# Two attention blocks in one kernel: value tiles cut in halves by heads, a separate stretch for each query tile of the last turn, and another written order of the work

## The chip, the cores and the metric

One core of one Trainium2 chip runs the whole kernel. The metric is the device time of one execution in microseconds. Three runs of the kernel before are shown, and one more execution was taken with the hardware profiler on.

## The reference

Two attention blocks work on 2048 tokens of width 640 each, with 32 heads of 20 columns. Their outputs stand side by side in a result of 2048 x 1280. Everything is bf16.

```
# A: four segments of 512 tokens, one after the other
logits = q @ k.T * 20**-0.5 + where(query < key, -1e9, 0)   # causal within a segment
a_dot  = softmax(logits) @ v
a_mem  = phi(q) @ M / (phi(q) @ z + 1e-6)       # phi(t) = t+1 if t > 0 else exp(t)
out    = (sigmoid(beta) * a_mem + (1 - sigmoid(beta)) * a_dot) @ wo
M += phi(k).T @ v ;  z += sum(phi(k))           # memory of the segments before
# B: sliding window, a query sees itself and the 255 keys before it
out    = softmax(where(0 <= i - j < 256, q @ k.T * 20**-0.5, -1e9)) @ v @ wo
```

## The kernel before

The work is cut into eight chunks of 512 tokens, which alternate: A0, B0, A1, B1, A2, B2, A3, B3 (numbers 0 to 7). For each chunk q and k are projected in five pieces of 128 columns (q, k with 32 rows per head of which 20 are the head's; the columns of the last heads are packed into the unused rows, written to DRAM and read back into groups 5 to 7), v in two halves of 16 heads, four token tiles each. Heads go in 8 groups of four. Scores are computed transposed (keys on partitions), 153 batches of up to 2 x 1024 columns in three two-bank tiles `sc`; ScalarE takes their exponentials into ten `pt` tiles (line 830), GpSimd (869) and VectorE (847) mask the edges. A value group (`av`, line 883; in the last chunk `av_tile`, line 904, by query tiles) multiplies the weights with v, which carries a column of ones for the sums. The result is transposed by 32 x 32 blocks on VectorE (949), divided on GpSimd (987), collected in `o`, written to DRAM, turned by a DMA transpose (1040) and projected with wo (935). In block A from segment 1 on a memory group is added (`mem`).

The matmuls of the projections, the value groups and the memory all go through two one-bank PSUM tiles `m0` and `m1`, used in turn. The output projections of the end use `sc` tiles too.

The values: `vA` (block A) and `vB0`, `vB1` (block B, by turns) are tiles of 128 partitions x 4 token tiles x 696 columns, which hold both halves of the heads of a chunk (line 789, `v_tile`). `vS` holds copies of vA with its 64-token blocks placed otherwise, `vL`, `vU` and `vX` copies of parts of vB for the edges of the window: `vL` the lower 64 tokens of each tile, `vU` the upper ones, `vX` the first tile with the other half from the chunk before. SyncE makes these copies by DMA (lines 757 and 783). For a chunk of B but the first, half 0 issues first the two carries from the chunk before (`vU` and `vX`, both halves of the heads at once), then three copies of its own half; half 1 issues three.

The turned rows: all chunks but the last turn their rows into `oT`; the last one, by query tiles, into a tile `xT` of 128 x 5 x 576, where query tile t takes the columns 128 t to 128 t + 127 of each of the five pieces (lines 1037 to 1041). Its last query tile is turned by matmuls instead (`last_job`).

What sets the order: TensorE runs in the order of the string `PLAN` (line 61). Each word is one step: `q20*5` five matmuls of q of chunk 2 from piece 0 on, `k`, `v`, `o` likewise (`v21`: half 1 of chunk 2; `o70`, `o71`, `o72`: query tiles of chunk 7), `S` or `s` one score batch, `A` one value group, `M` one memory group, `d2` a step of the update of the memory before chunk 2, `z0` the last query tile. After `S` the 128-column matmuls up to the next `A` are issued as four of 32 columns (`by_tiles`, line 930), after `s` as one. The order of the other engines follows from a planner (`Flow`, lines 96 to 267) that keeps a clock for each engine with fixed costs, releases an eviction, mask, division or DMA when it thinks that its input is there, and starts TensorE's next step when it thinks that it can. Only the order of the instructions comes from it; on the chip every engine runs its own list and waits on semaphores. A DMA waits also for the eighth one before it (eight lanes).

At the start SyncE loads x of chunk 0, pieces of the weights wk_A and wq_A (the first pieces on ScalarE's queue), beta, and wv_A in two halves, in this order. VectorE fills vL, vU and vX with zeros, GpSimd sets the ones of vA and vB.

Of the kernel before, what the change touches and what calls it, by code (L numbers as in the profile page):

```python
# [13 lines left out]
P = 128  # L14
# [253 lines left out]
class _K:  # L268
# [391 lines left out]
    def dm_job(self, seg, pkT, v):  # L660
# [12 lines left out]
        for some in (own, [(lambda kt, h=h: spare[:, kt, R2 * h:R2 * h + R2], R2,  # L673
                            [x for x in range(4) if MEM2[x][0] == h], None) for h in (1, 0)]):
            if some is not own:
                yield there
            yield "bank"
            dM, bi = self.bank()
            at = 0
            for lhs, rows, xs, g0 in some:  # L680

                gs = [g0] if g0 is not None else sorted(MEM2[x][1] for x in xs)
                n = W * len(gs)
                v0 = at_head(4 * gs[0])
                for kt in range(LT):
                    nc.tensor.matmul(dM[0:rows, at:at + n], lhsT=lhs(kt),  # L686
                                     rhs=v[:, kt, v0:v0 + n],
                                     start=(kt == 0), stop=(kt == LT - 1))
# [26 lines left out]
    def v_job(self, n, half, w_ap, v, gate, needs):  # L715
# [5 lines left out]
        for tt in range(LT):  # L721
            yield "bank"
            ps, bi = self.bank()
            for kt in range(self.KT):
                self.wide(ps, xT[:, kt, x0 + tt * P:x0 + (tt + 1) * P],
                          w_ap[:, half, kt, :], 320, kt == 0, kt == self.KT - 1)
                if kt < self.KT - 1:
                    yield 0.0
            src = ps[:, 0:320].rearrange("p (h e) -> p h e", e=DH)
            dst = v[:, tt, HV * half:HV * half + 16 * VS].rearrange(  # L730
                "p (h e) -> p h e", e=VS)[:, :, 0:DH]
            if gate:
                nc.vector.tensor_tensor(
                    out=dst, in0=src,
                    in1=self.omg[:, 16 * half:16 * half + 16].unsqueeze(2)
                    .to_broadcast([P, 16, DH]), op=ALU.mult)
# [10 lines left out]
    def v_squares(self, n, half, v):  # L747
# [3 lines left out]
        s = slice(HV * half, HV * half + HV)  # L751
        tok = v[0:SH, :, s].rearrange("p (a b) c -> p a b c", b=2)
        t = f.dve + 138.0

        def go():
            for odd in (0, 1):
                self.nc.sync.dma_start(
                    out=self.vS[SH * odd:SH * odd + SH, odd * 2:odd * 2 + 2, s],
# [6 lines left out]
    def v_ends(self, n, c, half, v):  # L765
# [4 lines left out]
        s = slice(HV * half, HV * half + HV)  # L770
# [18 lines left out]
    def v_tile(self, name, now=True):  # L789
        v = self.big.tile([P, LT, VW], BF16, name=name)  # L790
        if now:
            self.v_ones(v)
        return v

    def v_ones(self, v):
        self.nc.gpsimd.memset(
            v[:].rearrange("p t (x c) -> p t x c", x=2)[:, :, :, 0:16 * VS].rearrange(
                "p t x (h e) -> p t x h e", e=VS)[:, :, :, :, DH], 1.0)
        for c0 in (HV - 12, VW - 12):
            self.nc.gpsimd.memset(v[:, :, c0:c0 + 12], 1.0)  # L800
# [73 lines left out]
    def av(self, parts, g, vof):  # L874
# [4 lines left out]
        for n_, (ref, q0, nq, c0, pts) in enumerate(parts):  # L879
            v = vof(ref)  # L880
            for j in range(4):
                h = 4 * g + j
                nc.tensor.matmul(O[HD * j:HD * j + HD, q0:q0 + nq],  # L883
                                 lhsT=v[:, at_head(h):at_head(h) + HD],
# [7 lines left out]
    def av_tile(self, parts, qt, g0, vof):  # L892
# [3 lines left out]
        for gi in range(4):  # L896
            own = sorted((p[:5] for p in parts[g0 + gi] if p[1] // P == qt),
                         key=lambda e: -e[2])
            for n_, (ref, q0, nq, c0, pts) in enumerate(own):
                v = vof(ref)  # L900
                o0 = gi * P + q0 - qt * P
                for j in range(4):
                    h = 4 * (g0 + gi) + j
                    nc.tensor.matmul(O[HD * j:HD * j + HD, o0:o0 + nq],  # L904
                                     lhsT=v[:, at_head(h):at_head(h) + HD],
# [107 lines left out]
    def final(self, n, o, scr, wo, out2d, r0, col, t0, t1, t):  # L1013
# [19 lines left out]
        def turn(tl):  # L1033
            if n not in self.oT:
                if n == len(self.chunks) - 1:

                    self.oT[n] = self.big.tile([P, self.KT, XC], BF16, name="xT", bufs=2)
                else:
                    self.oT[n] = self.big.tile([P, self.KT, L], BF16, name="oT", bufs=2)
            nc.sync.dma_start_transpose(out=self.oT[n][:, :, t0 * P:t1 * P],  # L1040
# [7 lines left out]
    def final_job(self, n, wo, out2d, r0, col, t0, t1, there):  # L1048
# [4 lines left out]
        for tt in range(t0, t1):  # L1053
            if n == len(self.chunks) - 1 and tt == LT - 2:

                row = r0 + tt * P
                for hf in range(2):
                    yield "bank"
                    self.last_half(hf, lambda m: oT[:, m, tt * P:(tt + 1) * P], wo,
                                   out2d[row:row + P], col)  # L1060
# [7 lines left out]
            lhs = lambda m: oT[:, m, tt * P:(tt + 1) * P]  # L1068
# [235 lines left out]
    def body(self, xA, A_wq, A_wk, A_wv, A_wo, A_beta, xB, B_wqkv, B_wo, out2d):  # L1304
# [39 lines left out]
        self.vL = big.tile([P, LT, VW], BF16, name="vL")  # L1344
        self.vU = big.tile([P, LT, VW], BF16, name="vU")
        self.vX = big.tile([P, VW], BF16, name="vX")
        self.vA = self.v_tile("vA")
        self.vS = big.tile([P, LT, VW], BF16, name="vS")
        self.consts_mz()
        nc.vector.memset(self.vL[:].bitcast(F32), 0.0)  # L1350
        for t in (self.vU, self.vX):
# [6 lines left out]
        nc.gpsimd.memset(self.vS[:].bitcast(F32), 0.0)  # L1358
# [209 lines left out]
    def one_group(self, n, kind, c, g, what, parts, left, o_t, groups_done, scro, wo, out2d):  # L1568
# [3 lines left out]
        def vof(ref):  # L1572
            what, u = ref
            if what == "a":
                return self.vA[:, u, :]
            if what in "st":
                return self.vS[:, 2 * (u % 2) + u // 2, :]
            if what == "l":
                return self.vL[:, u % LT, :]
            if what == "u":  # L1580
                return self.vU[:, u + 2, :]
            if u == 0:
                return self.vX[:]
            return self.vB[c % 2][:, u, :] if u > 0 else self.vB[(c - 1) % 2][:, LT + u, :]
# [128 lines left out]
```

## Time and profile before

| what | value |
| --- | --- |
| median of 3 runs | 329.36 us (328.75 to 333.11) |
| profiled execution | 329.68 us, of which the span is 328.0 us |
| TensorE clock granted | 1.00 throughout |
| DMA packets | 76266, 47.45 MB, mean 145 GB/s |
| score exponentials on ScalarE | 306 of mean 1024 ns |
| GpSimd masks | 512 of mean 376 ns |
| 32 x 32 transposes on VectorE | 88 of mean 709 ns |

The span runs from the first to the last instruction; the rest of an execution lies around it. The profile names a group of instructions by its line, engine and operation and by what it writes and reads (`m<-xT,wBq`). PE is TensorE's matmuls and PEld its weight loads, DVE is VectorE, ACT ScalarE, POOL GpSimd, SP SyncE, and a q behind the name is the queue that issues DMAs. A list of waits gives, for an engine's line and what it waited for, the total in us, how many times, and the longest. "Issue" is time in which the engine waited for nothing that the profile shows. Matmuls are pipelined, so a busy share of TensorE includes overlap.

### The profile page before, as it was taken

How to read it: one execution, taken by the hardware profiler on the slowest of the kernel's cores; microseconds unless marked ns; L12 is line 12 of the kernel's file. 1: busy time of each engine (PE TensorE's matmuls, PEld its weight loads, DVE VectorE, ACT ScalarE, POOL GpSimd, SP SyncE). 2: the span in 40 equal slices, each digit the busy share in tenths (PEclk: the TensorE clock that was granted, in tenths of full speed). 3: DMA queues.
4: the chain of work that ended last, by engine and by line, in shares of the span. 5: the costliest groups of instructions: out<-in, count | busy, mean ns of one | idle time of the engine just before them, and what ended most of it. 6: DMA issues, size and time to landing. Idle time of an engine off the chain costs nothing. (4 is left out here: it accounts for less than half of the span.)

```text
span 328.0 us, 16968 instructions
## 1 busy us (share of the span) xinstructions
PE 315.8 (96%) x7195; PEld 176.3 (54%) x7195; DVE 255.6 (78%) x533; ACT 299.5 (91%) x333; POOL 265.3 (81%) x672
## 2 busy tenths in 40 slices
PE   8999999999999999999999999999999999999995
PEld 2454546555544455555654545456655445666663
DVE  6777767789877887998877897988776788876763
ACT  2979999999999998989999999899999999979982
POOL 8466689998769899977885999998976899998761
PEclk9999999999999999999999999999999999999999
DMA  7975845773689566164689146116968126587752
GB/s 207 400 253 124 199 142 90 162 199 64 137 222 182 108 161 180 38 138 145 142 218 170 28 87 156 52 26 133 156 184 194 26 48 157 141 203 186 119 122 88
DMA packets 76266, 47.45 MB, mean 145 GB/s; under 512 B 48382, under 2 KB 73182, under 8 KB 76190
## 3 DMA queue, kind: packets, MB, share of 16 engines
q1 hardware_dynamic: 75469, 45.71, 58.5%
q8 instruction: 56, 0.92, 1.2%
q10 hardware_dynamic: 720, 0.66, 0.7%
q14 instruction: 21, 0.16, 0.2%
HBM read 17.62 MB, written 16.96 MB: 105 GB/s over the span
## 5 line engine op out<-in xcount | busy, mean ns | idle before, releaser
L830 ACT ACTIVATE pt<-sc 128x1024 bf16<-128x1024 f32 (+2 forms) x306 | 282.5, 1024 | 14.4 <-PE sc L814 12.4
L869 POOL TENSOR_SCALAR_AFFINE_SELECT pt<-pt 128x128 bf16<-128x128 bf16 (+1 forms) x512 | 178.0, 376 | 48.9 <-ACT pt L830 42.0
L949 DVE STREAM_TRANSPOSE tt<-m 128x512 f32<-128x512 f32 x88 | 61.2, 709 | 24.9 <-PE m L883 16.1
L987 POOL TENSOR_TENSOR o<-tt,rr 128x320 bf16<-128x320 f32 x64 | 48.4, 757 | 3.6 <-DVE rr L977 2.6
L814 PE MATMUL sc<-qB,kB 20*64 20x64 bf16 (+2 forms) x1728 | 39.6, 217 | 1.0 <-ACT pt L830 0.3
L935 PEld LDWEIGHTS <-xT 128*128 128x128 bf16 x296 | 26.7, 97 | 18.3 <-issue 6.5
L847 DVE TENSOR_TENSOR pt<-pt,ends 128x1024 bf16<-128x1024 bf16 (+2 forms) x50 | 36.3, 737 | 0.0
L1100 DVE CAST ot<-m 128x320 bf16<-128x320 f32 x58 | 28.1, 486 | 9.4 <-PE m L935 8.2
L814 PEld LDWEIGHTS <-kB 20*64 20x64 bf16 (+1 forms) x1728 | 22.0, 98 | 22.5 <-issue 20.7
L814 PE MATMUL sc<-qA,kA 20*64 20x64 bf16 (+4 forms) x1024 | 33.4, 237 | 0.3 <-ACT pt L830 0.3
L935 PEld LDWEIGHTS <-oT 128*128 128x128 bf16 x244 | 21.4, 97 | 11.9 <-issue 2.6
L814 PEld LDWEIGHTS <-kA 20*128 20x128 bf16 (+1 forms) x1024 | 13.5, 97 | 22.2 <-issue 21.1
L935 PE MATMUL m<-wBv,xT 128*128 128x320 bf16 x147 | 24.2, 299 | 0.9 <-DVE tt L949 0.4
L883 PE MATMUL m<-pt,vA 128*32 128x192 bf16 (+3 forms) x512 | 23.6, 274 | 0.2
L935 PE MATMUL m<-xT,wBq 128*128 128x512 bf16 x82 | 21.4, 380 | 0.3 <-DVE tt L949 0.3
L935 PE MATMUL m<-wo_A,oT 128*128 128x320 bf16 x125 | 21.0, 301 | 0.3 <-DVE kA L557 0.3
L935 PE MATMUL m<-xT,wBk 128*128 128x512 bf16 x81 | 20.7, 381 | 0.0
L935 PE MATMUL m<-wv_A,xT 128*128 128x320 bf16 x119 | 19.8, 300 | 0.7 <-issue 0.5
L738 DVE CAST vB<-m 128x320 bf16<-128x320 f32 x32 | 15.6, 489 | 5.3 <-PE m L935 3.1
L935 PE MATMUL m<-wo_B,oT 128*128 128x320 bf16 x109 | 18.6, 300 | 0.6 <-DVE tt L949 0.4
L557 DVE CAST qB<-m 128x512 bf16<-128x512 f32 x20 | 13.8, 688 | 6.7 <-PE m L935 3.4
L557 DVE CAST kB<-m 128x512 bf16<-128x512 f32 x20 | 13.6, 681 | 6.6 <-PE m L935 5.6
(127 smaller groups left out, 464.1 us busy)
## 6 DMA issues: line engine op xcount, KB each, us to landing
out_dram<-ot SPq DMA_DIRECT2D x29, 160.0 KB
scr_o<-o SPq DMA_DIRECT2D x28, 160.0 KB
xT<-in_B_x_dram SPq DMA_DIRECT2D x8, 288.0 KB
xT<-in_A_x_dram SPq DMA_DIRECT2D x8, 256.0 KB
scr_pk<-e SPq DMA_DIRECT2D x15, 128.0 KB
vS<-vA SPq DMA_DIRECT2D x16, 87.0 KB
vL<-vB SPq DMA_DIRECT2D x8, 174.0 KB
scr_kA<-kA SPq DMA_DIRECT2D x16, 60.0 KB
```

What stands on the lines that cost most here:

```text
L557: nc.vector.tensor_copy(out=dst[:, m, at:at + L], in_=ps[:, :])
L738: nc.vector.tensor_copy(out=dst, in_=src)
L814: nc.tensor.matmul(ps[j // 2][h0:h1, j % 2, c0:c0 + nq], lhsT=k[rows, g, k0:k0 + h1 - h0], rhs=q[rows, g, q0:q0 + nq], start=True, stop=Tr ...
L830: nc.scalar.activation(out=pt[:, :, lo:hi], in_=ps[i][:, :, lo:hi], func=ACT.Exp, scale=self.scale)
L847: nc.vector.tensor_tensor(out=blk, in0=blk, in1=self.ends[:, c0, :].unsqueeze(1).unsqueeze(1) .to_broadcast([P, 2, n // SH, SH]), op=ALU.mult)
L869: nc.gpsimd.affine_select(out=blk, in_=blk, pattern=pat, compare_op=ALU.is_ge, fill=self.zero, base=base, channel_multiplier=mul)
L883: nc.tensor.matmul(O[HD * j:HD * j + HD, q0:q0 + nq], lhsT=v[:, at_head(h):at_head(h) + HD], rhs=pts[j // 2][:, j % 2, c0:c0 + nq], start= ...
L935: self.nc.tensor.matmul(ps[:, 0:n], lhsT=lhsT, rhs=rhs, start=start, stop=stop, skip_group_check=True)
L949: self.nc.vector.transpose(out=tt[:], in_=O[:, :])
L987: nc.gpsimd.tensor_tensor(out=to[:] if add_to else to, in0=a, in1=b, op=ALU.mult)
L1100: nc.vector.tensor_copy(out=ot[:, 320 * hf:320 * hf + 320], in_=ps[:, 0:320])
```

## The change

Three things are done at once.

Value tiles: `vA`, `vB0`, `vB1`, `vS`, `vL`, `vU` and `vX` become two tiles each, one for each half of the heads (348 columns). Readers choose the tile by the group (`g // 4`). The fills at the start become two each. The carries from the chunk before are issued by each half for itself, so that half 1 issues five copies instead of three and half 0's carries are half as large.

Turned rows: in the last chunk, query tile t takes the 640 columns from 640 t on of the flat tile `xT`, so that each query tile has a stretch of its own.

Order: `PLAN` has the same steps in another order, with other places of `S` and `s`.

```diff
 PLAN = (
-    "k00*5 q00*5 k01*4 S k01 q01*5 S v00*16 S v00*4 k02 S k02*4 k03*5 q02*3 S q02*2 q03*5 k04*5 "
+    "q00*5 k00*5 k01*5 v00*4 S v00 q01*5 v00*2 s v00*13 k02 s k02*4 q02*2 s q02*3 k03*3 S k03*2 "
...
-    "v71 s v71*4 A M s v71*10 s A M s o30*10 s o40*5 o30*5 s o30*5 A s o40*10 s o40*10 A o40*5 "
-    "s o40*5 o50*3 s o50*2 o40*5 o50*2 s o50*3 A s o50*10 s A o50*2 s o50*9 s o50*9 s A o60*5 s "
-    "o60*5 o70*5 A o70 s o70*4 o60*5 s o60*5 o71*4 s o71*6 o60*2 s o60*6 A o60*8 A o60*4 o72*2 "
-    "z0*4 ")
+    "v71*3 s v71 o30*5 A s v71*5 M s o40*5 A M s v71*8 s v71*2 o40*5 o30*5 s o40*5 A s o30*10 "
+    "o40*4 s o40*6 A o40*4 s o40*11 s o50*8 s A o50 s o50*11 s A o50 s o50*8 s o50*11 s A "
+    "o60*10 s o60*5 A o70*2 s o70*8 s o60*5 o71*5 s o71*5 o60*5 s o60*5 A o60*6 A o60*4 o72 "
+    "z0*2 o72 z0*2 ")
...
     def v_squares(self, n, half, v):
-        tok = v[0:SH, :, s].rearrange("p (a b) c -> p a b c", b=2)
+        tok = v[half][0:SH].rearrange("p (a b) c -> p a b c", b=2)
...
     def v_ends(self, n, c, half, v):
-        if half == 0 and c > 0:
-            pv = self.vB[(c - 1) % 2]
-            todo += [(self.vU[hi, 0:2, :], pv[hi, 2:4, :], 820.0),
-                     (self.vX[lo, :], pv[lo, 0, :], 410.0)]
-        todo += [(self.vL[lo, :, s], v[lo, :, s], 820.0),
-                 (self.vU[hi, 2:4, s], v[hi, 0:2, s], 410.0),
-                 (self.vX[hi, s], v[hi, 0, s], 205.0)]
+        if c > 0:
+            pv = self.vB[(c - 1) % 2][half]
+            todo += [(vU[hi, 0:2, :], pv[hi, 2:4, :], 410.0), (vX[lo, :], pv[lo, 0, :], 205.0)]
+        todo += [(vL[lo], v[lo], 820.0), (vU[hi, 2:4, :], v[hi, 0:2, :], 410.0),
+                 (vX[hi, :], v[hi, 0, :], 205.0)]
...
+    def half_tiles(self, name, ones=False):
+        ts = [self.big.tile([P, LT, HV], BF16, name="%s%d" % (name, x)) for x in range(2)]
+        for t in ts if ones else ():
+            self.nc.gpsimd.memset(t[:, :, 0:16 * VS].rearrange(
+                "p t (h e) -> p t h e", e=VS)[:, :, :, DH], 1.0)
+            self.nc.gpsimd.memset(t[:, :, HV - 12:HV], 1.0)
+        return ts
...
     def av(self, parts, g, vof):
-            v = vof(ref)
+            v = vof(ref, g // 4)
...
     def final(self, n, o, scr, wo, out2d, r0, col, t0, t1, t):
-                    self.oT[n] = self.big.tile([P, self.KT, XC], BF16, name="xT", bufs=2)
+                    t = self.big.tile([P, self.KT, XC], BF16, name="xT", bufs=2)
+                    flat = t[:].rearrange("p k s -> p (k s)")
+                    self.oT[n] = [flat[:, self.D * x:self.D * x + self.D].rearrange(
+                        "p (k s) -> p k s", k=self.KT) for x in range(LT)]
...
     def body(self, xA, A_wq, A_wk, A_wv, A_wo, A_beta, xB, B_wqkv, B_wo, out2d):
-        self.vL = big.tile([P, LT, VW], BF16, name="vL")
+        self.vL = self.half_tiles("vL")
...
-        self.vB = [self.v_tile("vB0"), self.v_tile("vB1")]
+        self.vB = [self.half_tiles("vB0", True), self.half_tiles("vB1", True)]
```

More of the change, by code (lines that the diff above doesn't have):

```diff
@@ L683, in dm_job @@
                 n = W * len(gs)
-                v0 = at_head(4 * gs[0])
+                v0 = at_head(4 * gs[0]) - HV * (gs[0] // 4)
                 for kt in range(LT):
                     nc.tensor.matmul(dM[0:rows, at:at + n], lhsT=lhs(kt),
-                                     rhs=v[:, kt, v0:v0 + n],
+                                     rhs=v[gs[0] // 4][:, kt, v0:v0 + n],
                                      start=(kt == 0), stop=(kt == LT - 1))
@@ L729, in v_job @@
             src = ps[:, 0:320].rearrange("p (h e) -> p h e", e=DH)
-            dst = v[:, tt, HV * half:HV * half + 16 * VS].rearrange(
+            dst = v[half][:, tt, 0:16 * VS].rearrange(
                 "p (h e) -> p h e", e=VS)[:, :, 0:DH]
@@ L750, in v_squares @@
         f = self.f
-        s = slice(HV * half, HV * half + HV)
-        tok = v[0:SH, :, s].rearrange("p (a b) c -> p a b c", b=2)
+        tok = v[half][0:SH].rearrange("p (a b) c -> p a b c", b=2)
         t = f.dve + 138.0
@@ L757, in go @@
                 self.nc.sync.dma_start(
-                    out=self.vS[SH * odd:SH * odd + SH, odd * 2:odd * 2 + 2, s],
+                    out=self.vS[half][SH * odd:SH * odd + SH, odd * 2:odd * 2 + 2, :],
                     in_=tok[:, :, odd, :])
@@ L769, in v_ends @@
         lo, hi = slice(0, SH), slice(SH, P)
-        s = slice(HV * half, HV * half + HV)
+        vL, vU, vX, v = self.vL[half], self.vU[half], self.vX[half], v[half]
         todo = []
-        if half == 0 and c > 0:
-            pv = self.vB[(c - 1) % 2]
-            todo += [(self.vU[hi, 0:2, :], pv[hi, 2:4, :], 820.0),
-                     (self.vX[lo, :], pv[lo, 0, :], 410.0)]
-        todo += [(self.vL[lo, :, s], v[lo, :, s], 820.0),
-                 (self.vU[hi, 2:4, s], v[hi, 0:2, s], 410.0),
-                 (self.vX[hi, s], v[hi, 0, s], 205.0)]
+        if c > 0:
[3 more added lines that the diff above has]
+                 (vX[hi, :], v[hi, 0, :], 205.0)]
         t = f.dve + 138.0
@@ L787, in v_ends @@
         f.at(t, go)
[L789 to L800, printed above, removed]
+    def half_tiles(self, name, ones=False):
[5 more added lines that the diff above has]
+        return ts
     def score_batch(self, n, ent, kof, q, masks):
@@ L899, in av_tile @@
             for n_, (ref, q0, nq, c0, pts) in enumerate(own):
-                v = vof(ref)
+                half = (g0 + gi) // 4
+                v = vof(ref, half)
                 o0 = gi * P + q0 - qt * P
                 for j in range(4):
-                    h = 4 * (g0 + gi) + j
+                    at = at_head(4 * (g0 + gi) + j) - HV * half
                     nc.tensor.matmul(O[HD * j:HD * j + HD, o0:o0 + nq],
-                                     lhsT=v[:, at_head(h):at_head(h) + HD],
+                                     lhsT=v[:, at:at + HD],
                                      rhs=pts[j // 2][:, j % 2, c0:c0 + nq],
@@ L1035, in turn @@
                 if n == len(self.chunks) - 1:
-                    self.oT[n] = self.big.tile([P, self.KT, XC], BF16, name="xT", bufs=2)
+                    t = self.big.tile([P, self.KT, XC], BF16, name="xT", bufs=2)
+                    flat = t[:].rearrange("p k s -> p (k s)")
+                    self.oT[n] = [flat[:, self.D * x:self.D * x + self.D].rearrange(
+                        "p (k s) -> p k s", k=self.KT) for x in range(LT)]
                 else:
                     self.oT[n] = self.big.tile([P, self.KT, L], BF16, name="oT", bufs=2)
-            nc.sync.dma_start_transpose(out=self.oT[n][:, :, t0 * P:t1 * P],
+            to = self.oT[n]
+            nc.sync.dma_start_transpose(out=to[t0][:, :, :] if isinstance(to, list) else to[:],
                                         in_=scr[t0 * P:t1 * P, :])
@@ L1058, in final_job @@
                     yield "bank"
[L1059 removed]
+                    self.last_half(hf, lambda m: oT[tt][:, m, :], wo,
                                    out2d[row:row + P], col)
@@ L1067, in final_job @@
             ot, slot = self.piece("ot", NOT, 1, BF16, (P, 640))
-            lhs = lambda m: oT[:, m, tt * P:(tt + 1) * P]
+            if isinstance(oT, list):
+                lhs = lambda m: oT[tt][:, m, :]
+            else:
+                lhs = lambda m: oT[:, m, tt * P:(tt + 1) * P]
             if self.all_scored:
@@ L1343, in body @@
         self.pkT = big.tile([P, LT, D], BF16, name="pkT")
-        self.vL = big.tile([P, LT, VW], BF16, name="vL")
[L1345 to L1348, printed above, removed]
+        self.vL = self.half_tiles("vL")
+        self.vU = self.half_tiles("vU")
+        self.vX = [big.tile([P, HV], BF16, name="vX%d" % x) for x in range(2)]
+        self.vA = self.half_tiles("vA", True)
+        self.vS = self.half_tiles("vS")
         self.consts_mz()
-        nc.vector.memset(self.vL[:].bitcast(F32), 0.0)
-        for t in (self.vU, self.vX):
+        for t in self.vL + self.vU + self.vX:
             nc.vector.memset(t[:].bitcast(F32), 0.0)
         self.consts_mem()
-        self.vB = [self.v_tile("vB0"), self.v_tile("vB1")]
+        self.vB = [self.half_tiles("vB0", True), self.half_tiles("vB1", True)]
         nc.gpsimd.memset(self.kB[0][:, :, 0:SH], 0.0)
@@ L1357, in body @@
         self.consts_ends()
-        nc.gpsimd.memset(self.vS[:].bitcast(F32), 0.0)
+        for t in self.vS:
+            nc.gpsimd.memset(t[:].bitcast(F32), 0.0)
         f.on_pool(10500.0)
@@ L1570, in one_group, with vof @@
         nm = 2 if kind == "A" and c > 0 else 1
-        def vof(ref):
+        def vof(ref, half):
             what, u = ref
             if what == "a":
-                return self.vA[:, u, :]
+                return self.vA[half][:, u, :]
             if what in "st":
-                return self.vS[:, 2 * (u % 2) + u // 2, :]
+                return self.vS[half][:, 2 * (u % 2) + u // 2, :]
             if what == "l":
-                return self.vL[:, u % LT, :]
+                return self.vL[half][:, u % LT, :]
             if what == "u":
-                return self.vU[:, u + 2, :]
+                return self.vU[half][:, u + 2, :]
             if u == 0:
-                return self.vX[:]
-            return self.vB[c % 2][:, u, :] if u > 0 else self.vB[(c - 1) % 2][:, LT + u, :]
+                return self.vX[half][:]
+            return (self.vB[c % 2][half][:, u, :] if u > 0
+                    else self.vB[(c - 1) % 2][half][:, LT + u, :])
         if what != "mem":
```

4 lines of the change are left out of this document (2 added, 2 removed), and 35 rows, old and new, of the table PLAN.

## The prediction

> **What bounds the kernel now.** I read the busy shares first, then the waits of all engines, then those of TensorE alone, then the timeline of the first 18 us, and last the end of the chain of work.
>
> ```profile
> span 328.0 us, 16968 instructions
> ...
> PE 315.8 (96%) x7195; PEld 176.3 (54%) x7195; DVE 255.6 (78%) x533; ACT 299.5 (91%) x333; POOL 265.3 (81%) x672
> ```
>
> Two engines are nearly full: TensorE (96%) and ScalarE (91%), whose work is the exponentials. Which of them waits for the other is in the list of waits (total us, times, longest):
>
> ```profile
> PEld L814 <- issue: 41.8, 133, 0.4
> PEld L935 <- issue: 20.0, 75, 0.9
> ...
> ACT pt L830 <- PE sc L814: 12.4, 23, 2.0
> ```
>
> ScalarE waits 12.4 us for scores. The other way it is 0.6 us, in the list of TensorE's own waits:
>
> ```profile
> PE m L935 <- DVE tt L949: 1.3, 6, 0.3
> ...
> PE m L935 <- DMA xT<-in_A_x_dram: 0.6, 1, 0.6
> ...
> PE m L935 <- DVE vA L733: 0.6, 3, 0.2
> PE sc L814 <- ACT pt L830: 0.6, 3, 0.3
> ```
>
> So TensorE sets the time, in the order that PLAN writes down, and ScalarE follows close behind. "Issue" is mostly the price of going from one tile shape to another: between a score batch and a 128-column matmul the start times of the trace leave about 0.12 us more than the matmuls themselves. I added up the matmuls at the spacing of their undisturbed neighbours (0.136 us for 128x320, 0.215 us for 128x512) and the 338 changes of shape at their usual price: about 304 us. The remaining 21 us up to the end of TensorE's work are waits spread over the span: 2.9 us in the first twentieth, 0.5 to 1.9 in each other. No single wait is worth 2%, and two thirds of them (13.3 us) stand ahead of a matmul that fills one of the two one-bank tiles m0 and m1 again before VectorE has emptied it.
>
> The head of the timeline (start, length, engine):
>
> ```profile
> 3.76 0.41 SPq L319 DMA_DIRECT2D wv_A<-in_A_wv_dram  x1
> ...
> 5.52 0.81 PE L935 MATMUL m<-xT,wk_A 128*128 128x512 bf16 x3 [0.63 <-DMA xT<-in_A_x_dram]
> ...
> 8.32 0.40 PE L814 MATMUL sc<-qA,kA 20*128 20x448 bf16 x8
> ...
> 8.76 1.94 ACT L830 ACTIVATE pt<-sc 128x1024 bf16<-128x1024 f32 x2 [0.24 <-PE sc L814]
> ...
> 10.39 2.47 PE L935 MATMUL m<-wv_A,xT 128*128 128x320 bf16 x16
> ```
>
> The first half of wv_A is issued at 3.76 and read at 10.39 without a wait. The trace's landing events for it run from 8.24 to 9.30.
>
> The end, from the chain of work:
>
> ```profile
> 319.32 0.80 PE m L904 x64
> 320.12 0.65 PE sc L935 x4
> 320.77 1.37 PE m L935 x10
> 322.16 0.49 DVE oe L1160
> 322.65 0.61 DVE pq L1126
> 323.31 1.55 PE m L935 x10
> ```
>
> **The change, part by part.** The sum is made against the profiled execution: 329.68 us, of which 328.0 are span. The median shown is 329.36, 0.32 less; I take that off at the end.
>
> *Same work.* Counting the two instruction streams: the same 153 score batches, 64 value groups, 24 memory groups, and 7195 against 7213 matmuls. The 18 more are 6 projection steps done as four 32-column matmuls instead of one. Sets of four take 0.161 us (320 columns) and 0.240 us (512) against 0.136 and 0.215: 6 x 0.025 = +0.15. Changes of shape are 337 against 338: -0.13. Together 0.
>
> *The first score batch.* Old order: k00 (5 matmuls), q00 (5), 4 of k01, scores. New: q00, k00, all of k01, 4 of v00, scores. That q00 comes first costs nothing: wq_A lands at 4.77 instead of wk_A's 3.75, but both orders then stand until the pieces of x at 5.48 and 5.84 (the 0.63 us above). From 6.17 on, k00 and k01 take 10 x 0.215, to 8.32. Then v00 needs wv_A, landed at 9.30: 0.98 us of standing, with the first score batch queued behind it on TensorE and all of ScalarE behind that. The scores start near 9.30 + 4 x 0.136 + 0.12 = 9.96 instead of 8.32. Of these 1.64 us, 0.7 is work brought forward; 0.95 is lost. TensorE has no long wait on anything else behind it that would give this back. Low bound 0, if the weights land by 8.3 (the transfer rates say that their last bytes moved near 8.0), high bound 1.64; I take +0.95, by the landing events, which the waiting matmul goes by.
>
> *Filling the two banks again.* Laid out on the undisturbed spacing, the old order has 50 places of 299 in which less than 0.9 us of TensorE work lies between the last matmul into a bank and the next first one; the trace loses 7.7 us there, 0.10 us in the median. At the other 249 it loses 0.02 each. The new order has 62. 12 x (0.10 - 0.02) = +1.0. Bounds: 0, if VectorE is free at these places, and 12 x 0.29 = +3.5, the mean of the dearest kind (a bank turned by a transpose). The median, since most of the added ones are the 320-column kind at 0.14.
>
> *Value tiles in halves.* This could remove waits of one half for the other. In the trace no read of vA or vB waits for a DMA, and writes to vA wait 1.4 us in all, for matmuls; the waits of L883 on L733 (0.7 us of weight loads, 0.4 of matmuls) are recent evictions of that kind. I take 0, bounds -1.1 and 0. The halves cost three more fills on VectorE: 1218 ns for 1392 elements and 348 for 348 give 0.83 ns an element and 58 ns fixed, so 3 x 58 ns and three gaps of 0.24: the last fill ends near 6.5 instead of 5.6, against 6.37 for the first cast; 0.1 us, covered by the wait for wv_A, and +0.1 if that is gone. GpSimd's additional fills lie ahead of 9.85, its first mask. SyncE issues six more carries (vU and vX for half 1 of three chunks) at 0.61 us each: 3.7 us spread over three places on a queue that itself waits 26.9 us for o in two places. 0.
>
> *A stretch for each query tile.* The transposes into xT carry no wait for TensorE in the old order, and the two waits for them (0.6 and 0.3) are for their own landing. 0, with -0.8 as the bound.
>
> *The end.* The new order puts one half of o72 between the two parts of z0. In the old one TensorE stands 0.6 us before the last ten matmuls at 323.31, behind the casts of 322.16 and 322.65. The cast at 322.65 can start 0.2 sooner. After the last score batch 15 o60 steps remain instead of 18, but the last value tile still waits for the same masks. -0.2, bounds -0.6 and +0.4.
>
> *Runs of short matmuls.* The 22 score batches of 64 small matmuls take 0.50 us from first to last start at best and up to 0.95; together 2.7 us over the best. The new order has the same batches with other neighbours. I take 0, bounds -2.7 and +2.7.
>
> Sum: 329.68 + 0.95 + 1.0 - 0.2 = 331.4, and 0.32 less for the median: **331.1**.
>
> **The rivals.** *A: the order pays as it stands.* The weights of v00 land by 8.3 and the added tight places cost nothing; tail -0.2, xT -0.4, half of the 2.7: 329.36 - 0.2 - 0.4 - 1.3 = 327.5 at its best, 328.6 in its middle. For it: bytes near 8.0, and tight places that cost nothing at all in the trace (11 of 50 under 0.03). Against it: the landing events.
>
> *B: the last chunk's value half lands late.* Place: the first value tile that reads half 1 of chunk 7. Between the last matmul of v71 and that tile the old order has 11.0 us of undisturbed work, the new 7.0. Needed: 0.7 for the eviction, three issues at 0.61, or five if the carries are not away before, and a landing, by the nearest row 3.4 (scr_o<-o in the chain): 5.9 to 7.2. So it just fits; what is missing is lost one for one. SyncE is held at such places by up to 10 us (its row for vB). From a landing 5 us later than that, the time passes 335.9 and the change is slower by over 2%. Middle: 334. The Trainium skill (DMA: Bandwidth & Descriptors, Bandwidth) speaks for this rival: it says to batch transfers and that those under 64 KB are ruled by their descriptors, and the halved vX carry is 43.5 KB. The same page's fixed 2.0 us per transfer (stated for the GpSimd path, under the anatomy of one DMA) would be an estimate of 12 us for six more in line, 343 us; the rows of vU and vX show them issued back to back at 0.61 us and no TensorE wait behind them, so the trace does not agree that they add up.
>
> *C: the halves and stretches remove hidden waits worth more than 2%.* It would need 6.6 us; all waits of TensorE and its weight loads on VectorE evictions and transfers that could be false are under 2. About 322.5.
>
> **How the numbers follow.** Forecast 0.47 (331.1, own range 329.6 to 333), A 0.36 (328.6), B 0.14 (334), C 0.03. From 326.8 to 334.8 leaves out C, about a third of B and the ends: 1 to 2 in 10. Over 2% from 329.36 means below 322.8 or above 335.9, about what a measurement of this kernel can tell from no change. Faster 0.02, slower 0.06 (the upper part of B), the same 0.92.
>
> **What would show it.** Right: a wait of TensorE on wv_A of 0.7 to 1.1 us near 9, first exponential near 10.4 instead of 8.76; more waits on VectorE evictions in the first list; TensorE busy within 1 us of 315.8; the last ten matmuls without the 0.6 us before them. Wrong: v00 at 8.4 without a wait; fewer waits at the banks; a wait on vL, vU or vX of several us after the last value projection.

## The result and the profile after

| | before | after |
| --- | --- | --- |
| median of 22 runs each | 329.71 us | 331.65 us |
| profiled execution, its span | 329.68 us, 328.0 us | 331.24 us, 329.5 us |

The ratio of after to before is 1.0051, with a 95% interval from 1.0027 to 1.0075: slower by 0.5%, 0.9 to 2.5 us, which counts as no change at 2%. Forecast were 331.1 us and "the same". The medians are taken over all runs; the ratio and its interval leave out those in a slower state of the chip (one of the 22 after, at 335.42 us and a granted clock of 0.989).

The busy shares of after, from its page:

```profile
span 329.5 us, 17010 instructions
...
PE 316.8 (96%) x7213; PEld 176.2 (53%) x7213; DVE 257.6 (78%) x536; ACT 300.0 (91%) x333; POOL 266.0 (81%) x676
```

Nothing has become the bound that wasn't: TensorE 96%, ScalarE 91%. From the list of waits of all engines (total us, times, longest):

```profile
PEld L808 <- issue: 40.8, 127, 0.6
PEld L930 <- issue: 17.0, 73, 0.5
ACT pt L824 <- PE sc L808: 14.0, 24, 3.4
```

ScalarE's wait for scores has grown from 12.4 to 14.0, and its longest from 2.0 to 3.4: that is the start of the kernel. TensorE's own waits:

```profile
PE m L930 <- DMA wv_A<-in_A_wv_dram: 1.5, 1, 1.5
...
PE m L930 <- DVE tt L944: 0.8, 4, 0.2
PE m L930 <- DMA xT<-scr_o: 0.7, 1, 0.7
PE sc L1124 <- POOL o L982: 0.7, 1, 0.7
```

The first line is the forecast wait, at 1.5 instead of 0.7 to 1.1 us. The waits for VectorE's transposes, of which the forecast wanted more, are fewer here (0.8 against 1.3). This list doesn't see most refills of the two banks. Their price can be read from start times alone: the two rows under "issue" are lower than before (41.8 and 20.0 there).

The head, from TensorE's and ScalarE's timelines (start, length, engine):

```profile
4.81 1.37 PE L930 MATMUL m<-xT,wq_A 128*128 128x512 bf16 x5 [0.56 <-DMA wq_A<-in_A_wq_dram]
6.02 2.32 PE L930 MATMUL m<-xT,wk_A 128*128 128x512 bf16 x10
9.85 0.72 PE L930 MATMUL m<-wv_A,xT 128*128 128x320 bf16 x4 [1.51 <-DMA wv_A<-in_A_wv_dram]
10.50 0.40 PE L808 MATMUL sc<-qA,kA 20*128 20x448 bf16 x8
```

```profile
10.93 1.94 ACT L824 ACTIVATE pt<-sc 128x1024 bf16<-128x1024 f32 x2 [3.40 <-PE sc L808]
```

TensorE is through with k01 at 8.3 and stands until wv_A has landed (last landing event 9.80; 9.29 in the trace of before). The first exponential starts 2.2 us later than before. The end:

```profile
321.93 0.84 PE L930 MATMUL m<-wo_B,xT 128*128 128x320 bf16 x5
323.43 0.40 PE L1124 MATMUL sc<-one,o 128*128 128x128 bf16 x4 [0.65 <-POOL o L982]
323.75 0.30 PE L1136 MATMUL sc<-one,o 128*32 128x32 bf16 x16
323.99 0.85 PE L930 MATMUL m<-wo_B,xT 128*128 128x320 bf16 x5
324.68 0.71 PE L930 MATMUL m<-wk_A,pq 128*128 128x320 bf16 x4
```

The half of o72 now fills the 0.56 us that stood before the last ten matmuls, but it is missing where it stood, and the first part of z0 waits 0.65 us for GpSimd's division instead.

Where the difference lies, by start times against the same undisturbed spacing as in the prediction (304.8 us of work before, 304.7 after; us of standing):

| kind | before | after |
| --- | --- | --- |
| up to 12 us (without warm-up) | 0.2 | 1.7 |
| refill of a bank with less than 0.9 us between | 7.7 | 8.7 |
| other refills | 5.5 | 5.4 |
| inside score batches of 64 short matmuls | 8.3 | 7.1 |
| rest | -0.8 | -0.5 |
| sum | 20.9 | 22.4 |

The sum moves by 1.5 us and the profiled executions by 1.56. (A row below zero means that the spacing assumed for those places was a little too large. The rows come from one execution of each kernel and from an assumed spacing, so they are not good to the tenth.)

### The profile page after: what moved, and what is told of

The parts are those of the page before. It is cut to its first block, busy times and chain, and to the rows that moved or that the text cites. A ratio compares the mean times of both kernels' runs of the same rounds, so it can differ in the third digit from the quotient of the medians.

```text
span 329.5 us, 17010 instructions
## 1 busy us (share of the span) xinstructions
PE 316.8 (96%) x7213; PEld 176.2 (53%) x7213; DVE 257.6 (78%) x536; ACT 300.0 (91%) x333; POOL 266.0 (81%) x676
## 4 chain that ended last, share of the span: by engine, by line
PE 74%; DVE 8%; POOL 7%; issue 3%; DMA 3%; ACT 2%; SPq 1%; POOLq 0%; ACTq 0%; DVEq 0%
PE m L930 38%; PE sc L808 15%; PE m L925 9%; PE m L877 9%; POOL pt L863 5%; DVE tt L944 3%; ACT pt L824 2%; DMA wv_A<-in_A_wv_dram 2%; PE m L899 2%; PE m L687 1%; DVE qA L558 1%; POOL o L982 1%; DVE ot L1102 1%; DVE pt L841 1%; DMA scr_pk<-e 1%
## 5 line engine op out<-in xcount | busy, mean ns | idle before, releaser
L930 PEld LDWEIGHTS <-xT 128*128 128x128 bf16 x289 | 25.8, 97 | 20.7 <-issue 6.1
L841 DVE TENSOR_TENSOR pt<-pt,ends 128x1024 bf16<-128x1024 bf16 (+2 forms) x50 | 35.4, 723 | 0.0
L930 PE MATMUL m<-wv_A,xT 128*128 128x320 bf16 x119 | 21.1, 300 | 1.5 <-DMA wv_A<-in_A_wv_dram 1.5
L930 PE MATMUL m<-xT,wBk 128*128 128x512 bf16 x83 | 22.3, 381 | 0.0
L930 PE MATMUL m<-xT,wBq 128*128 128x512 bf16 x78 | 19.9, 380 | 0.0
L930 PE MATMUL m<-wo_B,oT 128*128 128x320 bf16 x114 | 19.4, 300 | 0.1
L930 PE MATMUL m<-xT,wq_A 128*128 128x512 bf16 x74 | 18.8, 380 | 0.6 <-DMA wq_A<-in_A_wq_dram 0.6
```

What stands on the lines that cost most here:

```text
L841: nc.vector.tensor_tensor(out=blk, in0=blk, in1=self.ends[:, c0, :].unsqueeze(1).unsqueeze(1) .to_broadcast([P, 2, n // SH, SH]), op=ALU.mult)
L930: self.nc.tensor.matmul(ps[:, 0:n], lhsT=lhsT, rhs=rhs, start=start, stop=stop, skip_group_check=True)
```

## The experiments

Two theories stood at the start. Theory 1, the prediction's: the order costs, at the head and at the added tight refills, and the new tiles are worth nothing. Theory 2: what the head loses is given back on the way, and the cost arises later. Theory 3 was that the halves with their six more carries cost. Theory 4, that each whole value tile brings its own wait into the new order, came out of the second run. All ratios are against the kernel before on the same chip; the changed kernel stands at 1.0051.

**Scores first in the changed kernel.** In PLAN only:

```diff
-    "q00*5 k00*5 k01*5 v00*4 S v00 q01*5 v00*2 s v00*13 ...
+    "q00*5 k00*5 k01*5 S q01*5 v00*7 s v00*13 ...
```

> The changed kernel with one edit: at the start the first score batch comes before the first value projection (q00, k00, k01, scores, then q01 and v00), so that nothing before the first scores needs wv_A. Theory 1 (the wait for wv_A is paid in full): the first scores start near 8.4 us instead of 10.5, TensorE's wait for wv_A is gone, and the time falls by 0.95 to 1.5 us, to 330.2 to 330.7 where the changed kernel is 331.65. Theory 2 (a loss at the start is given back by ScalarE's waits and bank waits before the end): the first scores come just as early, and the time stays within 0.4 us of 331.65. Theory 3 (the halves and carries cost, not the order): as theory 2.

Measured: 331.37 us, ratio 1.0046 (1.0020 to 1.0072), so 0.2 us less than the changed kernel, give or take 1.2. The first scores start at 8.47 instead of 10.50, and the wait for wv_A is gone:

```profile
8.47 0.40 PE L806 MATMUL sc<-qA,kA 20*128 20x448 bf16 x8
...
9.88 1.38 PE L928 MATMUL m<-wv_A,xT 128*128 128x320 bf16 x7
```

I followed TensorE's lag behind the undisturbed layout in both profiles: the 1.2 us won after 12 us of work shrink to 0.5 after 60 (most of it in one stop of 0.46 us inside a score batch, of a kind that the last section comes back to), to 0.3 after 200, and are a loss of 0.8 at the end. But this profile is of an execution of 332.11 us, 0.7 over the run's median. Theory 2 fits better; the interval does not exclude a gain of 1 us.

**The new order on the old tiles.** The kernel before with the new PLAN string and nothing else.

> The kernel before with the changed kernel's PLAN and nothing else: value tiles whole, turned rows in one tile. Theories 1 and 2 (the order costs, the halves and stretch are free): 331.3 to 331.9, as the changed kernel. Theory 3 (halves and carries cost the 1.9 us): 329.7. If the order was only free of waits thanks to the halves, this kernel comes out above 332.

Measured: 346.29 us, ratio 1.0457 (1.0405 to 1.0509). All theories so far fall here: the new order by itself costs 4.6%, and the tiles take 13.4 us of it away (0.0406 x 329.7, give or take 1.9). VectorE's waits in this run:

```profile
DVE vA L733 <- DMA vS<-vA: 6.5, 1, 6.5
...
DVE vB L738 <- DMA vU<-vB: 3.4, 2, 3.0
```

Its timeline around the first, TensorE's, and SyncE's queue at the same time:

```profile
239.81 0.49 DVE L733 TENSOR_TENSOR vA<-m,omg 128x320 bf16<-128x320 f32 x1
...
247.52 0.49 DVE L733 TENSOR_TENSOR vA<-m,omg 128x320 bf16<-128x320 f32 x1 [6.54 <-DMA vS<-vA]
```

```profile
248.07 1.52 PE L930 MATMUL m<-wo_A,oT 128*32 128x320 bf16 x20 [5.75 <-DVE vA L733]
```

```profile
239.22 1.85 SPq L517 DMA_DIRECT2D kA<-scr_kA  x4
241.12 1.75 SPq L517 DMA_DIRECT2D qA<-scr_qA  x4
242.91 0.34 SPq L626 DMA_DIRECT2D pq<-scr_pq  x1
243.35 2.08 SPq L757 DMA_DIRECT2D vS<-vA  x2
```

The new PLAN mixes the halves (`... v61*5 ... v61 S v61*4 o30*5 S v60*5 A v60*2 s v60*3 ... v61*5`): half 0 is finished at 239.6 and is to be copied into vS; the third token tile of half 1 is projected from 240.4 on. In one tile, its eviction counts as a write over what the copy of half 0 still reads, though the columns differ. The copy stands in SyncE's queue behind nine other transfers, VectorE behind the copy, and TensorE 5.75 us behind VectorE. In the old PLAN every half 0 is complete before half 1 begins. The second wait, of 3.0 us, needs no mixing: in chunk 3 half 0 is complete first in both orders, but the new PLAN ends the first token tile of v31 20 steps behind the last step of v30, the old one 34, and the copy is not out by then. In the changed kernel the eviction into vA has no such wait:

```profile
234.91 0.49 DVE L734 TENSOR_TENSOR vA<-m,omg 128x320 bf16<-128x320 f32 x1
...
236.33 0.49 DVE L734 TENSOR_TENSOR vA<-m,omg 128x320 bf16<-128x320 f32 x1 [0.25 <-PE m L930]
```

**The new tiles with the old order.** The changed kernel with the old PLAN string.

> The changed kernel with the PLAN of the kernel before: value halves and a stretch for each query tile, old order. Theories 1 and 2 (halves and stretch cost and bring nothing): 329.4 to 330.0, within 0.3 us of the kernel before. Theory 3 (six more carries and three more fills cost): 331 to 331.7. If the halves and the stretch remove hidden waits: 329.0 or less, at most 0.8 us from the stretch and 1.1 us from the halves.

Measured: 330.84 us, ratio 1.0003 (0.9965 to 1.0041). On the old order, halves and stretch are worth nothing, within 1.3 us. Theory 3 falls.

**v00 brought forward in the kernel before.**

```diff
-    "k00*5 q00*5 k01*4 S k01 q01*5 S v00*16 S v00*4 ...
+    "q00*5 k00*5 k01*5 v00*4 S v00 q01*5 S v00*11 S v00*4 ...
```

> The kernel before with one edit: the start of its PLAN is put as in the changed kernel (q00, k00, all of k01, four matmuls of v00, then the first scores); the rest of the order, the tiles and the turned rows are as before. Theory 1: a wait of TensorE for wv_A of 0.7 to 1.6 us near 9, first scores near 10 to 10.5 instead of 8.3, and the time rises by 0.95 to 1.5 us, to 330.7 to 331.2 where the kernel before is 329.71. Theory 2 (given back): the same late first scores, and a time within 0.4 us of 329.71.

Measured: 331.35 us, ratio 1.0034 (1.0006 to 1.0061), 1.1 us more. The first scores start at 9.58, behind a wait for wv_A of 0.54 us only, since the weights landed sooner in this execution (last event 8.89). The lag behind the kernel before is 1.2 us after 12 us of work and 1.1 at the end: in this execution the head is paid in full, as theory 1 has it, and little of it is given back.

**The stretch undone.** In the changed kernel:

```diff
-                    flat = t[:].rearrange("p k s -> p (k s)")
-                    self.oT[n] = [flat[:, self.D * x:self.D * x + self.D].rearrange(
-                        "p (k s) -> p k s", k=self.KT) for x in range(LT)]
+                    self.oT[n] = [t[:, :, P * x:P * x + P] for x in range(LT)]
```

> The changed kernel with the turned rows of the last chunk as before (query tile t in columns 128 t on of one tile), value halves and new order kept. Found so far: the new order on the old tiles takes 346.3 us, with waits of 6.5 and 3.0 us of value evictions for copies of the other half. Theory 4 (the value halves alone take these waits away, the stretch does nothing): 331 to 332.3, as the changed kernel. Rival (the stretch does it, or a part): between 333 and 346.

Measured: 332.26 us, ratio 1.0066 (1.0044 to 1.0089): 0.5 us over the changed kernel, give or take 1.1. The 13.4 us are not the stretch's.

**B's value tiles whole.** For vB, vL and vU, and likewise for vX, while vA and vS stay cut and the copies are issued as in the changed kernel:

```diff
-        ts = [self.big.tile([P, LT, HV], BF16, name="%s%d" % (name, x)) for x in range(2)]
+        w = self.big.tile([P, LT, 2 * HV], BF16, name=name)
+        ts = [w[:, :, HV * x:HV * x + HV] for x in range(2)]
```

> The changed kernel, but the value tiles of block B (vB, vL, vU, vX) are whole again, both halves in one tile; vA and vS stay cut. Theory 4 (each tile that is whole brings back its own wait: an eviction of one half stands behind the copy of the other): the wait of the eviction into vB for vU's copy near 114 us is back with 3 us or more, that of vA for vS near 241 is not, and the time is 335 to 338 (4.2 us were lost near 105 to 117 in the run with all tiles whole, 7.6 near 235 to 248). Rival (the loss comes from the six more carries being absent or from the other order of SyncE's queue): no such split, either 331.7 or above 343.

Measured: 335.49 us, ratio 1.0162 (1.0129 to 1.0196), 3.7 us over the changed kernel. VectorE's timeline has the wait where it was expected:

```profile
112.30 0.68 DVE L845 TENSOR_TENSOR pt<-pt,ends 128x1024 bf16<-128x1024 bf16 x1
116.23 0.49 DVE L739 CAST vB<-m 128x320 bf16<-128x320 f32 x1 [3.25 <-DMA vU<-vB]
```

**Block A's value tiles whole.** The same edit for vA and vS, with B's cut.

> The changed kernel, but vA and vS are whole again, both halves in one tile; the value tiles of block B stay cut (the counterpart of the run with B's tiles whole, which cost 1.1% over the changed kernel). Theory 4 (each whole tile brings back its own wait): the eviction into vA waits 5 us or more for vS's copy near 240, no wait for vU near 114, and the time is 338 to 341; the two costs together make up the new order on the old tiles, 346. Rival: under 334, the wait of vA then came only through the wait of vB before it.

Measured: 339.42 us, ratio 1.0292 (1.0259 to 1.0324), 7.9 us over the changed kernel, with this among VectorE's waits:

```profile
DVE vA L734 <- DMA vS<-vA: 6.7, 1, 6.7
```

The two prices add up to 11.6 of the 13.4 us; the rest is within the error of these differences (about 2 us). Theory 4 stands: in the new order the whole tiles of each block bring back their own wait.

**The middle of the new order alone.** Steps 404 to 789 of PLAN from the changed kernel, the rest from the kernel before, on the new tiles.

> The changed kernel's tiles with the PLAN of the kernel before, except for its steps 404 to 789 (from about 104 to 203 us), which are the changed kernel's. Theory 2 (the new order loses at the start and at the end, and gains 1.3 to 2 us in the middle: its lag behind the kernel before goes from 2.0 us at 100 to 0.3 at 203): 327.9 to 328.7, below both kernels. Theory 1 (the loss is spread over the added tight bank refills and nothing is gained anywhere): 329.7 to 330.3.

Measured: 330.42 us, ratio 1.0001 (0.9973 to 1.0029). The gain is there and does not last: in the profile TensorE is 1.2 us ahead of the kernel before after 200 us of work, and level with it after 240 (some 15 us later by the clock of the trace). VectorE's timeline on the way, first of this run, then of the kernel before:

```profile
238.20 0.49 DVE L1100 CAST ot<-m 128x320 bf16<-128x320 f32 x1 [0.41 <-PE m L928]
238.62 0.73 DVE L839 TENSOR_TENSOR pt<-pt,ends 128x1024 bf16<-128x1024 bf16 x1
239.54 0.69 DVE L839 TENSOR_TENSOR pt<-pt,ends 128x1024 bf16<-128x1024 bf16 x1 [0.18 <-ACT pt L822]
240.15 0.88 DVE L1100 CAST ot<-m 128x320 bf16<-128x320 f32 x2
```

```profile
239.70 0.74 DVE L847 TENSOR_TENSOR pt<-pt,ends 128x1024 bf16<-128x1024 bf16 x1
240.40 0.49 DVE L1100 CAST ot<-m 128x320 bf16<-128x320 f32 x1
240.81 0.68 DVE L847 TENSOR_TENSOR pt<-pt,ends 128x1024 bf16<-128x1024 bf16 x1
241.41 0.91 DVE L1100 CAST ot<-m 128x320 bf16<-128x320 f32 x2
```

With TensorE's order altered earlier, the planner has put both edge masks ahead of the evictions. The second mask waits for ScalarE's exponential, the eviction behind it for the mask, and TensorE for the eviction: 0.72 us by its row in the timeline, 0.88 by start times. What TensorE had won ahead of ScalarE, it hands back here.

**The new end alone.** The old PLAN up to step 789, then the new, on the new tiles.

> The changed kernel's tiles with the PLAN of the kernel before up to step 789 (203 us) and the changed kernel's order from there to the end. Theory 2: the end costs 1.1 to 1.6 us, so 330.8 to 331.4 where the kernel before is 329.7. Theory 1 (head and bank refills spread evenly): 0.3 to 0.6 us over the kernel before, 330.0 to 330.4.

Measured: 335.23 us, ratio 1.0150 (1.0112 to 1.0188), 4.9 us more, which no theory said. In the profile the lag behind the kernel before is 1.1 us after 180 us of work, though the order up to there is the same, 2.8 after 230, and 4.0 at the end. The last part, 1.2 us, is what theory 2 expected of the end; the 1.7 us in the middle come around the seam (by start times 0.75 us for an eviction at 220, and a stop of 0.94 inside a score batch at 231) and are not found in either whole order. So stretches of these two orders can't be priced by cutting them together.

**wv_A on ScalarE's queue.** In the changed kernel:

```diff
         self.wA["q"] = self.load_qk("wq_A", A_wq, 0, 1, nc.scalar)
+        self.wv_A = self.load_w("wv_A", A_wv, None, 6000.0, None, nc.scalar)
+        self.loads.pop(0)[1]()
...
-                self.wv_A = self.load_w("wv_A", A_wv, None, 6000.0)
-                self.loads.pop(0)[1]()
```

> The changed kernel, order kept, but the first half of wv_A is loaded on ScalarE's queue right behind the first piece of wq_A, some 2 us earlier than on SyncE's queue behind beta. Theory 1 (the wait for wv_A is paid in full): the wait of 1.5 us shrinks to 0 to 0.5 and the time falls by 0.9 to 1.5 us, to 330.2 to 330.8 where the changed kernel is 331.65. Theory 2 (what is gained at the start is given back to later waits, as in the run with the scores first): the wait shrinks as much, the time stays within 0.4 us of 331.65.

Measured: 332.70 us, ratio 1.0097 (1.0065 to 1.0129), 1.5 us over the changed kernel. The head:

```profile
5.47 1.08 PE L931 MATMUL m<-xT,wq_A 128*128 128x512 bf16 x4
7.32 0.38 PE L931 MATMUL m<-xT,wq_A 128*128 128x512 bf16 x1 [0.77 <-DMA xT<-in_A_x_dram]
...
9.70 0.71 PE L931 MATMUL m<-wv_A,xT 128*128 128x320 bf16 x4
10.33 0.40 PE L809 MATMUL sc<-qA,kA 20*128 20x448 bf16 x8
```

The wait for wv_A is gone, but a piece of x now lands later, so that q00's last matmul starts at 7.32 instead of 5.8, and the planner adds three warm-up matmuls (0.6 us). The scores start at 10.33 instead of 10.50. The run moved the wait and did not remove it, so it says nothing on whether a loss at the head is given back. Nor is the head what makes it slower: after 20 us TensorE is 0.1 us ahead of the changed kernel, and at 24 it is 1.0 behind. This wait does not stand in the changed kernel's list:

```profile
PE m L878 <- DVE tt L945: 0.9, 1, 0.9
```

With the head altered, the planner has put four small VectorE operations on kA ahead of the transpose that empties a value group's bank, which starts 1.5 us later (23.57 instead of 22.06), and TensorE's next group waits for it.

**Without VectorE's edge masks.** In both kernels the 50 multiplications by `ends` are left out of the computation, all other instructions in their order:

```diff
-                nc.vector.tensor_tensor(
-                    out=blk, in0=blk,
-                    in1=self.ends[:, c0, :].unsqueeze(1).unsqueeze(1)
-                    .to_broadcast([P, 2, n // SH, SH]),
-                    op=ALU.mult)
```

> The changed kernel without the 50 edge masks that VectorE multiplies in block B (left out of the computation; every other instruction stays in its order). VectorE loses 35 us of its 258. Theory 1 (tight bank refills wait for a busy VectorE): TensorE's stalls at refills fall from 15.8 by 3 us or more, the time to 326 to 329, and the distance to the kernel before without the same masks shrinks to the head's 1.0 us. Theory 2 (the two orders differ in how ScalarE, GpSimd and the DMAs are met, not in VectorE's load): the distance stays 1.5 to 2.3 us. If nothing waits for VectorE: 331 to 332.

> The kernel before without the same 50 edge masks, every other instruction in its order. Theory 1: stalls at refills fall from 13.3 by 2 to 3 us, time 325.5 to 328. Theory 2: as much below the kernel before as the changed kernel without masks is below the changed one. If nothing waits for VectorE: 329.4 to 330.

Measured: changed kernel 330.15 us, ratio 1.0012 (0.9991 to 1.0034), 1.3 us less than with masks, give or take 1.1; kernel before 329.73 us, ratio 1.0001 (0.9978 to 1.0025), no less than with masks. The distance between the two orders goes from 0.51% to 0.11%, give or take 0.32. VectorE's busy time falls by 30 us in each (257.6 to 227.7 in the changed kernel, 255.6 to 225.1 in the kernel before). The standing at refills falls from 14.1 to 12.3 us in the changed kernel and from 13.2 to 10.5 before: less than the 3 us expected of the first, and most of it remains without the masks. The times suggest that the new order suffers more from a loaded VectorE, at the edge of the noise (the distance shrinks by 0.40%, give or take 0.40); the refills do not show it, so where the 1.3 us sit stays open.

## Why the prediction came out right, and where it was wrong

*Same work, 0:* right (304.8 against 304.7 us of undisturbed work; TensorE busy 316.8 against 315.8).

*First score batch, +0.95:* the mechanism is right, the size short. The place cost 1.5 us in the trace, because the landing, taken from one execution at 9.30, came at 9.80; in another kernel with the same loads it was near 8.9. Brought into the old order the step costs 1.1 us; taken out of the new one it brings 0.2 (each give or take about 1). The two do not exclude each other (a price of 0.7 fits both), so whether anything behind the head gives this back stays open.

*Filling the banks again, +1.0:* right at the tight places (7.7 to 8.7) and nothing at the others; that it is right to the tenth is luck, from one execution of each. The list of waits, by which it was to be seen, does not show it.

*Value halves, 0:* this is the step that failed, though the sum did not. On the old order they are worth 0, as argued (0.1 us, give or take 1.3). On the new one they are worth 13.4 with the stretch, 11.6 of it found by making A's and B's tiles whole. The waits that they take away do not exist in the trace of before, where no eviction waits for a copy. The prediction priced the parts one by one against the old trace; its 0 for the halves was luck, and came out only because both parts were changed together. What the diff itself said was not used: the new PLAN alternates `v60` and `v61`, and brings `v31` nearer to `v30`.

*Stretch, 0:* not told apart from 0 (0.5 us, give or take 1.1). *The end, -0.2:* the gap before the last ten matmuls closed as said, and a wait of 0.65 us for GpSimd opened ahead of z0. From the last four wo_A matmuls to the start of the last one it is 4.49 us before and 4.59 after: +0.1.

*Runs of short matmuls, 0 with bounds of 2.7:* -1.2 in the trace, so the sum of the terms (1.5 + 1.0 - 1.2, and 0.2 over all else, the end included) came to 1.5 where 1.75 was forecast.

Rival A (the order pays) failed at the head; rival B (a value half too late) did not happen, and six more carries cost nothing that can be measured. With B went the reading of the Trainium skill (DMA: Bandwidth & Descriptors, Bandwidth) that small transfers ought to be batched: here the six transfers more cost nothing that can be measured (0.1 us on the old order, give or take 1.3). Nor is it the splitting of transfers that the new order needs: with B's tiles whole they were issued in the same halves, and the wait stood. Rival C asked for hidden waits above 2% in the old order; there are none.

## What to carry to other kernels

Before you price the parts of a change one by one, ask which part allows which: a tile cut in two can be worth nothing in the old order and 4% in the new, and a trace of the old order cannot show it. In a tuned order, time won by one engine can be handed back where another engine's fixed queue puts its eviction behind other work (0.7 us with the middle alone, 0.9 with wv_A loaded early); test a local gain by the whole kernel's time, not by the stretch. A landing read from one execution is known to about half a microsecond (8.89, 9.29 and 9.80 here).

## What the runs showed of the hardware

A stop of TensorE can slow what follows. In the run with whole tiles, the windows around the wait of 5.75 us (columns: window, its length, busy time of PE, PEld, DVE, ACT and POOL with counts, the granted TensorE clock, DMA share, GB/s):

```profile
240.00:248.00 8.00, 2.32 (x69) 1.46 (x67) 1.27 (x4) 3.25 (x4) 3.92 (x10) 0.82 0.60 162
248.00:250.00 2.00, 1.93 (x74) 1.15 (x75) 1.00 (x3) 0.00 (x0) 0.00 (x0) 0.50 0.00 0
250.00:252.00 2.00, 2.00 (x39) 1.22 (x31) 0.49 (x3) 1.65 (x2) 0.73 (x1) 0.51 0.28 95
252.00:254.00 2.00, 2.00 (x25) 1.12 (x22) 2.00 (x5) 1.22 (x3) 0.00 (x0) 1.00 0.16 31
```

The clock is at half for some 4 us after the stop, which makes 7.6 us out of a wait of 5.75 (7.6 is the growth of the lag between 220 and 230 us of work). A much shorter stop does it too. In the kernel before without masks, one score batch breaks off with no wait that the profile knows:

```profile
291.48 0.61 PE L814 MATMUL sc<-qB,kB 20*64 20x64 bf16 x52
293.99 0.25 PE L814 MATMUL sc<-qB,kB 20*64 20x64 bf16 x12 [1.90 <-issue]
```

```profile
292.00:294.00 2.00, 0.10 (x14) 0.01 (x3) 0.24 (x2) 0.00 (x0) 1.62 (x4) 1.00 0.91 190
294.00:296.00 2.00, 2.00 (x34) 1.20 (x35) 0.49 (x1) 1.34 (x2) 0.00 (x0) 0.79 0.73 219
296.00:298.00 2.00, 2.00 (x20) 1.11 (x10) 0.49 (x1) 2.00 (x3) 0.41 (x2) 0.50 0.19 37
```

After 1.90 us of standing the clock went to 0.50; after the 1.51 us for wv_A in the changed kernel it stayed at 1.00. The clock in all fourteen traces draws the same line: each of the six stops of 1.89 us or more (1.89, 1.90, 2.23, 2.49, 5.61, 5.75) was followed by a stretch at half clock, and none of the shorter ones behind the first 6 us was. The half clock began 2.8 to 3.8 us after TensorE had stopped, so after a short stop it meets work that is already running again, and it lasted 3.4 us after the four short stops and 6.8 after the two long ones. The Trainium skill (TensorE: Matmul & The Clock Gate, Why this matters for your kernels) names gaps over some 3 us as the danger; the traces say that less is enough.

Breaks inside the batches of 64 short matmuls are of two kinds. One has its wait on record. Near 138 us TensorE stands after the same matmul in the changed kernel, with the scores first and without the stretch, 0.56 us each time from start to start, and it waits for ScalarE's exponential:

```profile
139.01 0.68 PE L808 MATMUL sc<-qB,kB 20*64 20x64 bf16 x62 [0.36 <-ACT pt L824]
```

The other kind stands under "issue", as the 1.90 us above do: 15 breaks in the fourteen traces, of 0.4 to 2.1 us from start to start. They come at six places of the instruction stream, and what they wait for can be read from the transfers. The page of the kernel before lists 56 packets of 16 KB on the queue named "instruction", one for 257 of TensorE's 14390 matmuls and weight loads. Counted in this stream, all 15 breaks lie 178 to 186 instructions behind a multiple of 256, and TensorE goes on 1.2 to 1.6 us after the latest of these packets has moved its last bytes. At the place near 293 that packet ended at 291.51 in the kernel before, and TensorE, there at 292.62, stood for 0.28 us; without masks TensorE came at 291.88, the packet ended at 292.61, and it stood for 2.11 (the 1.90 above, start to start). So TensorE seems to be out of instructions at these places. This rests on the coincidence in time and place; no run moved a packet.
